# A planned instruction order: keeping small matmul groups together on TensorE, with retuned planner numbers

## The chip, the cores and the metric

One Trainium2 chip, one of its cores. The metric is device time of one execution in microseconds (us); lower is better. The profile's engine names are PE (TensorE matmuls), PEld (its weight loads), DVE (VectorE), ACT (ScalarE), POOL (GpSimd) and SP (SyncE, which issues the DMAs).

## What is computed

A gated linear attention over 4 x 8 heads, 768 steps, head dimension 40, and then two feed-forward layers on the 3072 tokens of width 320 with inner width 2048. Everything is float32. Cut to what matters:

```python
# attention: one recurrence over time for each of the 32 heads
m_new = max(f_t + m, i_t)
C = exp(f_t + m - m_new) * C + exp(i_t - m_new) * outer(v_t, k_t)
n = exp(f_t + m - m_new) * n + exp(i_t - m_new) * k_t
y_t = sigmoid(o_t) * (C @ q_t) / max(|n . q_t|, 1)
# then, on x = y as (3072, 320)
h = x @ w_in          # (3072, 2048)
x = max(0.01 * h, h) @ w_out
h = max(x @ w_in2, 0)
out = (h * h) @ w_out2
```

## The kernel before

The 768 steps are cut into 6 chunks of 128. `attention(c)` does a chunk in closed form for 4 batches b and 2 halves of 4 heads, so 8 groups g = 2b + half. A group on PE is: `mS` (line 635, four 128x128 score products into the one bank `attS`), `mI` (645, the part that comes from the carried state, into the one bank `atty`; not in chunk 0), and `mPV` (651; from chunk 2 on `mPV3`, 657 to 660) into the same `atty`. Around them stand, once a chunk, the gate transposes (546, 547); for each pair of batches the state update `mU` (708, 16 products); for each batch the transpose of the result (750); and in chunk 0 a broadcast of the gates for each group (615). DVE multiplies scores and decay (638), splits operands into high and low parts (665) and combines (684 to 686, which frees `atty`); ACT does the exponentials (626). All these PE pieces are called small groups below: in them a weight tile of 128 columns serves a moving operand of 32 to 128 columns. All other work of PE is called big: `moe_h` (434) and `out1` (465 to 471) for the first layer, `moe_h` and `out2` (513 to 515) for the second. Their moving operand has 256 to 512 columns. Each fp32 product is made of fp32r products of high and low parts, so a block of `moe_h` is 8 matmuls.

The weights of both layers come from DRAM and are split in the kernel (`weight`, lines 387 to 413) by DVE and ACT; the 16 blocks of the first layer are needed from the first chunk on.

The order on every engine is fixed before the run by `Sched`. Each piece is a node with an engine, an estimated duration, a key (how urgent it is), and buffers with a limited number of slots. `forward()` plays the program: each free engine takes, of the nodes that are ready and can have their buffers, the one with the smallest key. `backward()` then replaces keys by latest start times, and this is done 6 times; the best plan is written out. The first keys come from the numbers of the table `ORDER`. When PE has nothing ready, early in the program, the planner inserts a filler: a matmul of zeros with 512 columns (322 writes `hp`, 478 adds zero to an accumulator). Three more products of zeros (461) clear the accumulators.

The choice in `forward()` that the change touches is:

```python
pick = None
for n in sorted(cand, key=lambda n: (n.key, n.seq)):
    if all(b.live or (b.first is n and ...) for b in n.bufs):
        pick = n
        break
```

On the chip each engine then runs its list in order; an instruction whose input is late holds up all behind it on its engine.

Of the kernel before, what the change touches and what calls it, by code (L numbers as in the profile page):

```python
# [30 lines left out]
ORDER = dict(pe0=7000, ld2=80, kv=-2.33, ks=6.4, g2=32.54, z=-15.1, lag=7, m0=0.71, o0=1.85, a04=-6.78, a0s=4.65, a1=29.4, a1s=5.72, a1ld=23.83, w0=-33.49, ws=2.64, bias=1.13, c0=-19.03, cs=13.0, cld=31.54, wl=1.51, outk=2.04)  # L31
SHARE = 0.6
PASSES = 6
# [13 lines left out]
class Node:  # L47
    __slots__ = ("eng", "dur", "fn", "key", "deps", "outs", "ndep", "ready", "allocs", "bufs", "end", "start", "table", "lat", "seq", "alt", "after", "first", "bank")


class Sched:
# [10 lines left out]
    def op(self, eng, dur, key, fn, r=(), w=(), table=None, lat=0, alt=None, after=0):  # L62
# [4 lines left out]
        n.eng, n.dur, n.fn, n.key, n.table, n.lat = eng, dur, fn, key, table, lat  # L67
# [24 lines left out]
        self.nodes.append(n)  # L92
        return n
# [43 lines left out]
    def forward(self):  # L137
# [17 lines left out]
        ready = {e: [] for e in self.SAME}  # L155
# [6 lines left out]
        out, now, dma_free, done, last = [], 0.0, 0.0, 0, 0.0  # L162
        while done < len(self.nodes):

            for e, cand in ready.items():
# [3 lines left out]
                for n in sorted(cand, key=lambda n: (n.key, n.seq)):  # L169
                    if all(b.live or (b.first is n and queue[b.tag][-1] is b and free[b.tag] > 0) for b in n.bufs):  # L170
                        pick = n
                        break
# [25 lines left out]
                dur = n.dur  # L198
                if n.table and n.table != table:
# [63 lines left out]
def mlstm_moe_kernel(  # L263
# [265 lines left out]
    def attention(c, keys, ld):  # L529
# [23 lines left out]
        op("PE", 380, k0, gate_T, r=[(G_sb, f"A{p}"), (G_sb, f"c{p}"), (G_sb, f"w{p}"), (ident, 0)], w=[(gp, 0)])  # L553
# [11 lines left out]
        for b in range(B):  # L565
# [33 lines left out]
            for hf in range(2):  # L599
# [9 lines left out]
                if c == 0:  # L609
# [7 lines left out]
                    op("PE", 4 * 214, key, bc, r=[(ident, 0), (G_sb, "A0"), (G_sb, "c0"), (G_sb, "w0")], w=[(ab, 0)])  # L617
# [19 lines left out]
                op("PE", 4 * (214 if native else 113), key + 0.3, mS, r=tk, w=[(sp, 0)])  # L637
# [3 lines left out]
                if c:  # L641
# [5 lines left out]
                    op("PE", 4 * (214 if native else 113), key + 0.35, mI, r=tk + ([(C32, (b, 0)), (C32, (b, 1))] if native else [(Cst, (b, k)) for k in range(3)]), w=[(py, 0)])  # L647
# [14 lines left out]
                if thirds:  # L662
# [9 lines left out]
                    op("PE", 4 * 126, key + 0.5, mPV3, r=[(pb, (pr, i)) for i in range(3)] + [(vb, (vr, i)) for i in range(3)], w=[(py, 0)])  # L672
                else:
                    op("PE", 4 * 214, key + 0.5, mPV, r=[(aw, 0), (nt, 0)], w=[(py, 0)])
# [25 lines left out]
            if c < NCH - 1 and b % 2:  # L700
# [9 lines left out]
                op("PE", 1170, kU, mU, r=[(x, 0) for _, wv, nt in pair for x in (wv, nt)], w=[(up, 0)])  # L710
# [41 lines left out]
            op("PE", 3 * 112, ko + 0.75, mT, r=[(y, 0), (y, 1), (ident, 0)], w=[(xp, 0)])  # L752
# [106 lines left out]
```

## Time and profile before

| | |
|---|---|
| median of 3 runs | 856.4 us (851.79 to 860.84) |
| the profiled execution | 857.15 us |
| its span, first to last instruction | 855.1 us |
| PE busy in the span | 842.0 us (98%) |
| DVE, ACT, POOL busy | 541.4, 464.9, 77.8 us |
[...]

Attention and the split of the first layer's weights lie in the first 440 us, on top of the first feed-forward layer; from about 440 us on only feed-forward work is left. A busy PE in the profile is not PE at its peak: the ends of matmuls are modelled and overlap the next, so the pace is read from the distance between starts.

### The profile page before, as it was taken

What the parts mean: (1) busy time and instruction counts of PE and PEld (TensorE: products, weight loads), DVE (VectorE), ACT (ScalarE), POOL (GpSimd) and SP (SyncE); (2) the same over time, 40 slices, a digit from 0 to 9 for tenths busy, and PEclk for the clock granted to TensorE, in tenths of its full rate; (3) what the DMA queues carried; (4) which work ended last, traced back from release to release, by engine and by line L of the source; (5) the groups of instructions that cost most, each with busy time, mean ns of one, the idle gap of its engine ahead of it and who ended that gap; (6) DMA issues with size and microseconds to landing.
All of it is one profiled execution on the core that took longest, in us unless ns stands there. A gap on an engine that the chain in (4) does not pass through costs nothing.

```text
span 855.1 us, 14028 instructions
## 1 busy us (share of the span) xinstructions
PE 842.0 (98%) x5310; PEld 729.9 (85%) x5310; DVE 541.4 (63%) x1008; ACT 464.9 (54%) x946; POOL 77.8 (9%) x101
## 2 busy tenths in 40 slices
PE   9899999999999999999999999999999999999998
PEld 7689999788778788788888889999999999999997
DVE  7799876767676776667576899453443443533433
ACT  6577638656765776577455675343333433433332
POOL 2231204103010311011000000000000000000000
PEclk8899999999999999999999999999999999999999
DMA  8675325435343543453232442000000000000000
GB/s 226 222 233 183 118 73 181 140 111 172 103 137 114 165 138 109 152 166 118 77 103 72 165 136 69 1 31 1 1 32 1 14 17 1 31 1 1 32 1 31
DMA packets 52211, 78.60 MB, mean 92 GB/s; under 512 B 4336, under 2 KB 40784, under 8 KB 52144
## 3 DMA queue, kind: packets, MB, share of 16 engines
q1 hardware_dynamic: 52144, 77.71, 28.8%
q8 instruction: 42, 0.69, 0.3%
q14 instruction: 25, 0.20, 0.1%
HBM read 54.26 MB, written 4.01 MB: 68 GB/s over the span
## 4 chain that ended last, share of the span: by engine, by line
PE 82%; DVE 6%; ACT 4%; SPq 3%; DMA 3%; issue 1%; ACTq 0%; DVEq 0%
PE hp L434 36%; PE acc L465 4%; PE acc L467 4%; PE acc L466 4%; SPq L581 3%; PE acc L515 3%; PE acc L514 3%; PE acc L513 3%; PE attS L635 3%; PE acc L470 2%; PE atty L645 2%; PE acc L471 2%; PE atty L651 2%; DMA T<-X 2%; PE atty L515 1%
## 5 line engine op out<-in xcount | busy, mean ns | idle before, releaser
L434 PE MATMUL hp<-xH,w 128*128 128x512 f32 (+1 forms) x1040 | 294.8, 381 | 0.3 <-DVE gL L442 0.3
L434 PEld LDWEIGHTS hp<-xH,w 128*128 128x128 f32 x1040 | 183.5, 189 | 29.2 <-DVE gL L442 0.9
L434 PE MATMUL hp<-xL,w 128*128 128x512 f32 (+1 forms) x624 | 199.1, 375 | 0.0
L446 DVE TENSOR_TENSOR g<-g 128x512 f32<-128x512 f32 x96 | 66.3, 691 | 118.4 <-ACT g L445 118.3
L434 PEld LDWEIGHTS hp<-xL,w 128*128 128x128 f32 x624 | 115.9, 189 | 22.4
L445 ACT ACTIVATE g<-hp 128x512 f32<-128x512 f32 x96 | 57.3, 597 | 129.4 <-PE hp L434 129.4
L448 DVE TENSOR_TENSOR gL<-g,gH 128x512 fp32r<-128x512 f32 x96 | 66.4, 692 | 56.4 <-ACT gH L447 56.4
L447 ACT CAST gH<-g 128x512 fp32r<-128x512 f32 x96 | 59.6, 620 | 70.4 <-DVE g L446 70.4
L442 DVE TENSOR_TENSOR gL<-hp,gH 128x512 fp32r<-128x512 f32 (+1 forms) x112 | 68.3, 610 | 34.7 <-ACT hp L441 34.2
L465 PE MATMUL acc<-gH,w 128*128 128x512 f32 (+1 forms) x224 | 86.1, 384 | 0.0
L440 ACT ACTIVATE gH<-hp 128x512 fp32r<-128x512 f32 (+1 forms) x112 | 59.6, 532 | 48.4 <-PE hp L434 39.3
L467 PE MATMUL acc<-gL,w 128*128 128x512 f32 (+1 forms) x224 | 81.3, 363 | 0.0
L466 PE MATMUL acc<-gH,w 128*128 128x512 f32 (+1 forms) x224 | 81.0, 362 | 0.0
L515 PE MATMUL acc<-w,gL 128*128 128x320 f32 x192 | 59.3, 309 | 0.0
L514 PE MATMUL acc<-w,gH 128*128 128x320 f32 x192 | 59.3, 309 | 0.0
L513 PE MATMUL acc<-w,gH 128*128 128x320 f32 x192 | 59.2, 308 | 0.0
L441 ACT ACTIVATE hp<-hp 128x512 f32<-128x512 f32 (+1 forms) x112 | 59.1, 528 | 0.0
L626 ACT ACTIVATE aw<-aw,cs 128x128 f32<-128x128 f32 x160 | 50.8, 391 | 12.2 <-DMA aw<-Adram 12.1
L629 POOL TENSOR_SCALAR_AFFINE_SELECT aw<-aw 128x512 f32<-128x512 f32 x48 | 33.5, 697 | 196.5 <-ACT aw L626 174.0
L467 PEld LDWEIGHTS acc<-gL,w 128*128 128x128 f32 x224 | 42.6, 190 | 6.9 <-DVE gL L442 0.2
L465 PEld LDWEIGHTS acc<-gH,w 128*128 128x128 f32 x224 | 42.7, 191 | 5.3
L466 PEld LDWEIGHTS acc<-gH,w 128*128 128x128 f32 x224 | 42.8, 191 | 4.9
(163 smaller groups left out, 1515.1 us busy)
## 6 DMA issues: line engine op xcount, KB each, us to landing
T<-X SPq DMA_DIRECT2D x144, 120.0 KB
x<-in_wts_dram SPq DMA_DIRECT2D x16, 704.0 KB
aw<-Adram SPq DMA_DIRECT2D x40, 256.0 KB
nat<-in_nat_dram SPq DMA_DIRECT2D x24, 328.0 KB
qkr<-in_qk_dram SPq DMA_DIRECT2D x16, 360.0 KB
X<-in_wts_dram SPq DMA_DIRECT2D x8, 704.0 KB
T<-in_wts_dram SPq DMA_DIRECT2D x8, 704.0 KB
og<-in_og_dram SPq DMA_DIRECT2D x12, 320.0 KB
```

The lines of the kernel that those rows point to most:

```text
L434: T.matmul(hp.t[:, 0:n], w.t[:, col:col + 128], x.t[:, kt, o], start=(s == 0), stop=(s == 7))
L440: op("ACT", act(n, True), key, lambda: A.activation(gH.t[:, 0:n], h(), AF.Prelu, alpha=0.01), r=[(hp, 0)], w=[(gH, 0)])
L442: op("DVE", dve(n), key, lambda: V.tensor_tensor(out=gL.t[:, 0:n], in0=h(), in1=gH.t[:, 0:n].bitcast(F32), op=ALU.subtract), r=[(hp, 0), ( ...
L446: op("DVE", dve(n), key, lambda: V.tensor_tensor(out=g.t, in0=g.t, in1=g.t, op=ALU.mult), r=[(g, 0)], w=[(g, 0)])
L447: op("ACT", act(n), key, lambda: A.copy(gH.t, g.t), r=[(g, 0)], w=[(gH, 0)])
L448: op("DVE", dve(n), key, lambda: V.tensor_tensor(out=gL.t, in0=g.t, in1=gH.t.bitcast(F32), op=ALU.subtract), r=[(g, 0), (gH, 0)], w=[(gL, 0)])
L465: T.matmul(a[t].t[:, o], w.t[:, hc:hc + 128], gH.t[:, 0:n], start=first, stop=False)
L466: T.matmul(a[t].t[:, o], w.t[:, lc:lc + 128], gH.t[:, 0:n], start=False, stop=False)
L467: T.matmul(a[t].t[:, o], w.t[:, hc:hc + 128], gL.t[:, 0:n], start=False, stop=last)
L513: T.matmul(a.t[:, 0:DM], gH.t[:, s], wH, start=first, stop=False)
L514: T.matmul(a.t[:, 0:DM], gH.t[:, s], wL, start=False, stop=False)
L515: T.matmul(a.t[:, 0:DM], gL.t[:, s], wH, start=False, stop=last)
```

## The change

The planner learns of small groups. Eight `op` calls get `small=True` (all the small groups named above). When a big piece follows a small one, the planner now counts 85 ns more for it. And when the last piece on PE was small and the best candidate is big, the planner goes on through the candidates, up to `STAY` = 3000 ns of key beyond the best, and takes a small one that is ready instead. Beside that, 14 numbers of `ORDER` are different. No instruction's own work changes; the line numbers of the attention part are 8 higher in the changed file.

```diff
-ORDER = dict(pe0=7000, ld2=80, ..., g2=32.54, z=-15.1, lag=7, m0=0.71, o0=1.85, a04=-6.78, a0s=4.65, a1=29.4, a1s=5.72, ..., w0=-33.49, ...)
+ORDER = dict(pe0=7535.6, ld2=74.38, ..., g2=29.83, z=-12.64, lag=5, m0=0.64, o0=2.08, a04=-9.44, a0s=4.65, a1=22.66, a1s=2.23, ..., w0=-42.16, ...)
+STAY = 3000
...
                     if all(b.live or (b.first is n and queue[b.tag][-1] is b and free[b.tag] > 0) for b in n.bufs):
-                        pick = n
-                        break
+                        if pick is None:
+                            pick = n
+                        elif n.small:
+                            pick = n
+                        if e != "PE" or pick.small or not small or n.key > pick.key + STAY:
+                            break
...
                 dur = n.dur
+                if e == "PE":
+                    dur += 85 if small and not n.small else 0
+                    small = n.small
...
-        op("PE", 380, k0, gate_T, r=[...], w=[(gp, 0)])
+        op("PE", 380, k0, gate_T, small=True, r=[...], w=[(gp, 0)])
...
-                op("PE", 4 * (214 if native else 113), key + 0.3, mS, r=tk, w=[(sp, 0)])
+                op("PE", 4 * (214 if native else 113), key + 0.3, mS, small=True, r=tk, w=[(sp, 0)])
```

Over the whole program PE's list has 119 places where a big matmul follows a small group before, and 106 now; products of zeros are 36 before (18 of line 322, 15 of 478, 3 of 461) and 33 now (22, 8, 3).

What this does to the lists is shown at three places. First, PE in chunk 0: the second score product of batch 1, the clearing of accumulators (line 461), fillers (322), and the value product of group 1 (651; the row with `atty` after the fillers). Before:

```order
L651 MATMUL atty<-nat,aw 128x42 x4
L635 MATMUL attS<-w_102 128x128 x4
L635 MATMUL acc_230<-w_105 128x128 x4
L461 LDWEIGHTS warm
L461 MATMUL acc_235<-warm 128x512
L461 LDWEIGHTS warm
L461 MATMUL acc_239<-warm 128x512
L651 MATMUL atty<-nat,aw 128x42 x4
L615 MATMUL attS<-G_sb,ident 128x128 x4
L322 LDWEIGHTS warm
L322 MATMUL hp<-warm 128x512
L651 MATMUL atty<-nat,aw 128x42 x4
```

The same place on PE now (lines are 8 higher: 659 is 651, 643 is 635, 469 is 461, 330 is 322):

```order
L643 MATMUL acc_229<-w_105 128x128 x4
L659 MATMUL atty<-nat,aw 128x42 x4
L469 LDWEIGHTS warm
L469 MATMUL acc_249<-warm 128x512
L330 LDWEIGHTS warm
L330 MATMUL hp<-warm 128x512
L469 LDWEIGHTS warm
L469 MATMUL acc_260<-warm 128x512
L330 LDWEIGHTS warm
L330 MATMUL hp<-warm 128x512
L330 LDWEIGHTS warm
L330 MATMUL hp<-warm 128x512
```

The value product of group 1 moved ahead of the zero products, and these now stand six in a row (one more, of line 486, follows the five shown; then the broadcast 623 and the value product of group 2). Ahead of all work of chunk 0 stand 19 fillers where 16 stood.

Second, DVE in chunk 0, from the normalisation of batch 0 (736 to 743) to that of batch 1; 394, 396 and 399 are three steps of the split of weight blocks 0 (`x_2`) and 1 (`x_3`). Before:

```order
L394 TENSOR_SCALAR x_2_289<-x_4_122 128x704
L738 RECIPROCAL d<-d 128x8
L363 TENSOR_TENSOR G_sb<-G_sb,x_0_74 32x128
L740 TENSOR_TENSOR og<-og,d 128x320
L361 COPY G_sb<-x_0_74 32x128
L743 TENSOR_TENSOR y<-hs,og 128x320
L396 SCALAR_TENSOR_TENSOR x_2_289<-x_4_122,x_2_289 128x704
L736 SCALAR_TENSOR_TENSOR d<-hs 128x8
L399 ISA x_2_289<-x_2_289,wl 128x1408
L756 TENSOR_TENSOR xL<-attm,xH 128x3x128
L737 TENSOR_SCALAR d<-d 128x8
L394 TENSOR_SCALAR x_3_338<-x_5_126 128x704
```

The same place on DVE now (402 is 394, 404 is 396, 407 is 399, 744 to 751 are 736 to 743):

```order
L745 TENSOR_SCALAR d<-d 128x8
L402 TENSOR_SCALAR x_3_291<-x_5_126 128x704
L746 RECIPROCAL d<-d 128x8
L370 TENSOR_TENSOR G_sb<-x_0_74 32x128
L748 TENSOR_TENSOR og<-og,d 128x320
L407 ISA x_2_245<-x_2_245,wl 128x1408
L751 TENSOR_TENSOR y<-hs,og 128x320
L404 SCALAR_TENSOR_TENSOR x_3_291<-x_5_126,x_3_291 128x704
L369 COPY G_sb<-x_0_74 32x512
L744 SCALAR_TENSOR_TENSOR d<-hs 128x8
```

The third step of block 0 and the first two of block 1 moved ahead of the row that starts the normalisation of batch 1 (the last row shown).

Third, PE after the fourth set of gate transposes, where the state update `mU` (708, now 716) stands. Before:

```order
L471 MATMUL acc_2902<-gL,w_386 128x512
L635 MATMUL attS<-T 128x128 x4
L708 MATMUL attm<-wv,nat 40x42 x16
L434 MATMUL hp<-xH,w_583 128x512 x4
L434 MATMUL hp<-xL,w_583 128x512 x2
```

The same place on PE now:

```order
L475 MATMUL acc_2890<-gL,w_406 128x512
L643 MATMUL attS<-T 128x128 x4
L653 MATMUL atty<-Cst,T 128x42 x4
L716 MATMUL attm<-wv,nat 40x42 x16
L643 MATMUL attS<-T 128x128 x4
L478 MATMUL acc_2899<-gH,w_406 128x512
```

Two score products now stand in one cluster with only `mI` and `mU` between them. This form (S, I, U, S) stands 2 times in the list before and 5 times now.

## Rows read from the trace of the kernel before

**Rows 1.** Busy time by stretch: stretch, length, engines (instructions), granted clock, DMA share, GB/s.

```profile
40.00:60.00 20.00, 19.63 (x170) 17.95 (x169) 19.51 (x40) 16.89 (x46) 6.49 (x8) 0.93 0.73 245
60.00:80.00 20.00, 19.70 (x157) 18.68 (x156) 19.63 (x43) 15.79 (x36) 3.58 (x5) 0.99 0.63 198
...
280.00:320.00 40.00, 38.91 (x271) 31.86 (x270) 29.95 (x60) 30.65 (x66) 9.64 (x12) 1.00 0.46 148
...
560.00:600.00 40.00, 40.00 (x225) 36.28 (x224) 17.69 (x27) 14.88 (x27) 0.00 (x0) 1.00 0.05 17
```

**Rows 2.** Timeline of PE, 0 to 36 us: start, duration, operation, count.

```profile
1.05 5.99 PE L322 MATMUL hp<-warm 128*128 128x512 bf16 x16 [1.05 <-DVE warm L319]
6.87 0.24 PE L546 MATMUL attS<-ident,G_sb 96*128 96x96 f32 x1
...
16.30 1.04 PE L461 MATMUL acc<-warm 128*128 128x512 bf16 x2
17.13 1.77 PE L651 MATMUL atty<-nat,aw 128*128 128x42 f32 x8
...
27.26 0.63 PE L478 MATMUL acc<-warm 128*128 128x512 bf16 x1
...
35.39 0.72 PE L434 MATMUL hp<-xH,w 128*128 128x256 f32 x4
```

**Rows 3.** Timeline of DVE, 0 to 36 us; in brackets the idle time before and its releaser.

```profile
5.01 0.28 DVE L363 TENSOR_TENSOR G_sb<-G_sb,x 32x128 f32<-32x128 f32 x1
...
27.83 0.17 DVE L736 SCALAR_TENSOR_TENSOR d<-hs 128x8 f32<-128x8 f32 x1 [3.67 <-ACT hs L682]
27.92 0.88 DVE L399 CUSTOM_DVE_ANT_0 x<-x,wl 128x1408 uint16<-128x1408 uint16 x1
...
29.62 0.52 DVE L394 TENSOR_SCALAR x<-x 128x704 int32<-128x704 int32 x1
...
30.18 0.89 DVE L396 SCALAR_TENSOR_TENSOR x<-x,x 128x704 int32<-128x704 int32 x1
```

**Rows 4.** Timeline of ACT, 7 to 50 us: the exponentials of one group in chunk 0.

```profile
35.73 1.14 ACT L626 ACTIVATE aw<-attS,cs 128x128 f32<-128x128 f32 x4 [1.27 <-PE attS L615]
```

**Rows 5.** Stretches of 1 us, columns as in rows 1.

```profile
15.00:16.00 1.00, 1.00 (x11) 1.00 (x10) 1.00 (x2) 1.00 (x1) 0.32 (x1) 1.00 0.74 234
16.00:17.00 1.00, 1.00 (x5) 0.53 (x4) 1.00 (x2) 0.98 (x3) 0.00 (x0) 0.54 0.65 184
...
29.00:30.00 1.00, 1.00 (x13) 0.25 (x13) 0.92 (x3) 0.72 (x2) 0.00 (x0) 0.63 0.06 23
...
57.00:58.00 1.00, 1.00 (x7) 1.00 (x7) 1.00 (x4) 0.61 (x2) 0.91 (x2) 0.52 0.72 209
```

**Rows 6.** Timeline of PE, 50 to 57 us: first row of a run of small groups, and what follows.

```profile
51.91 0.30 PE L546 MATMUL attS<-ident,G_sb 96*128 96x96 f32 x1
...
56.14 0.74 PE L434 MATMUL hp<-xH,w 128*128 128x256 f32 x4
```

**Rows 7.** Timeline of PE around two small groups at 212 us.

```profile
212.35 0.56 PE L635 MATMUL attS<-T 120*128 120x128 f32 x4
212.75 0.57 PE L645 MATMUL atty<-Cst,T 120*128 120x42 f32 x4
213.16 0.48 PE L465 MATMUL acc<-gH,w 128*128 128x512 f32 x1
213.48 0.39 PE L466 MATMUL acc<-gH,w 128*128 128x512 f32 x1
213.71 0.40 PE L467 MATMUL acc<-gL,w 128*128 128x512 f32 x1
```

**Rows 8.** Who waited for whom, PE, 100 to 460 us: total us, times, longest us.

```profile
PE atty L645 <- DVE hs L686: 2.7, 4, 0.8
PE atty L659 <- DVE x L665: 1.9, 3, 1.3
PE attS L635 <- DVE aw L638: 1.1, 2, 0.8
```

More of the change, by code (lines that the diff above doesn't have):

```diff
@@ L47 @@
 class Node:
-    __slots__ = ("eng", "dur", "fn", "key", "deps", "outs", "ndep", "ready", "allocs", "bufs", "end", "start", "table", "lat", "seq", "alt", "after", "first", "bank")
+    __slots__ = ("eng", "dur", "fn", "key", "deps", "outs", "ndep", "ready", "allocs", "bufs", "end", "start", "table", "lat", "seq", "alt", "after", "first", "bank", "small")
 class Sched:
@@ L60, in buf, with op @@
         return Buf(tag, make)
-    def op(self, eng, dur, key, fn, r=(), w=(), table=None, lat=0, alt=None, after=0):
+    def op(self, eng, dur, key, fn, r=(), w=(), table=None, lat=0, alt=None, after=0, small=False):
         n = Node()
         n.alt, n.after, n.first = alt, max(after, ORDER["pe0"]) if eng == "PE" and key > -2000 else after, (eng, dur, fn)
-        n.eng, n.dur, n.fn, n.key, n.table, n.lat = eng, dur, fn, key, table, lat
+        n.eng, n.dur, n.fn, n.key, n.table, n.lat, n.small = eng, dur, fn, key, table, lat, small
         n.seq, n.outs, n.allocs, n.end = len(self.nodes), [], [], None
@@ L161, in forward @@
                 heapq.heappush(at, (n.after, 1, n.seq))
-        out, now, dma_free, done, last = [], 0.0, 0.0, 0, 0.0
+        out, now, dma_free, done, last, small = [], 0.0, 0.0, 0, 0.0, False
         while done < len(self.nodes):
@@ L645, in mI @@
                             T.matmul(py.t[:, (8 + n) * E:(9 + n) * E], lhs(0, h), st, start=True, stop=True)
-                    op("PE", 4 * (214 if native else 113), key + 0.35, mI, r=tk + ([(C32, (b, 0)), (C32, (b, 1))] if native else [(Cst, (b, k)) for k in range(3)]), w=[(py, 0)])
+                    op("PE", 4 * (214 if native else 113), key + 0.35, mI, small=True, r=tk + ([(C32, (b, 0)), (C32, (b, 1))] if native else [(Cst, (b, k)) for k in range(3)]), w=[(py, 0)])
                 def mPV(py=py, aw=aw, v=v, hd=hd):
@@ L671, in attention @@
                        alt=("POOL", pool(512), lambda lw=lw: lw(G, 1)))
-                    op("PE", 4 * 126, key + 0.5, mPV3, r=[(pb, (pr, i)) for i in range(3)] + [(vb, (vr, i)) for i in range(3)], w=[(py, 0)])
+                    op("PE", 4 * 126, key + 0.5, mPV3, small=True, r=[(pb, (pr, i)) for i in range(3)] + [(vb, (vr, i)) for i in range(3)], w=[(py, 0)])
                 else:
-                    op("PE", 4 * 214, key + 0.5, mPV, r=[(aw, 0), (nt, 0)], w=[(py, 0)])
+                    op("PE", 4 * 214, key + 0.5, mPV, small=True, r=[(aw, 0), (nt, 0)], w=[(py, 0)])
                 def comb(py=py, hs=hs, hf=hf, g=g):
@@ L708, in mU @@
                             T.matmul(up.t[r:r + D, o:o + E], nt.t[:, h * D:(h + 1) * D], wv.t[:, h], start=True, stop=True)
-                op("PE", 1170, kU, mU, r=[(x, 0) for _, wv, nt in pair for x in (wv, nt)], w=[(up, 0)])
+                op("PE", 1170, kU, mU, small=True, r=[(x, 0) for _, wv, nt in pair for x in (wv, nt)], w=[(up, 0)])
                 for i, (b2, _, _) in enumerate(pair):
@@ L750, in mT @@
                     T.transpose(xp.t[:, k * 128:(k + 1) * 128], y.t[:, k * 128:(k + 1) * 128], ident.t)
[L752 removed]
+            op("PE", 3 * 112, ko + 0.75, mT, small=True, r=[(y, 0), (y, 1), (ident, 0)], w=[(xp, 0)])
             xo = slice(b * CH, (b + 1) * CH)
```

6 lines of the change are left out of this document (3 added, 3 removed).

## The prediction

> **What bounds the kernel now.** I read the stretches first, then the timelines of PE, DVE and ACT in the first 36 us, then the list of waits. From 560 to 600 us PE is busy for all 40.00 us while DVE has 17.69 [rows 1]: once attention is over, only the matmuls themselves count, and the change leaves each of them as it was. Time can move in three ways: PE starts its big work earlier or later, it loses less between its instructions, or it waits less for others. The first is decided before 35.39 us, where the first block of line 434 starts [rows 2]; until then PE runs a chain of small groups and zero products. From 40 to 80 us there are two busy engines: PE 19.63 and 19.70 of 20, DVE 19.51 and 19.63 [rows 1]. Waits of PE proper from 100 to 460 us are few: 2.7, 1.9 and 1.1 us in its three largest items [rows 8].
>
> The profiled execution took 857.15 us, 0.75 above the median of 856.4. The sum below goes onto 857.15; 0.75 comes off at the end.
>
> **Boundaries.** In a row of matmuls with 512 columns the starts are 0.23 us apart (213.48 to 213.71). The first one after a small group keeps 0.32 until the next (213.16 to 213.48): 0.09 more [rows 7]. Inside the cluster nothing of the kind shows: the score group takes 0.40 (212.35 to 212.75) and the group from the state 0.41 (212.75 to 213.16), so joining two groups saves one boundary and does not move its price inside. There are 13 boundaries fewer (119 to 106, counted in the lists): 13 x 0.09 = **-1.2 us**, on PE, which sets the end, so nothing hides it. The bounds are 0 (what is saved only lengthens a wait) and -1.2.
>
> [...]
>
> **The start, in four pieces.** (a) The gate chain of chunk 0 is done on DVE at 5.29 us (5.01 + 0.28) [rows 3], but the first transpose starts at 6.87, behind 16 zero products [rows 2]. Three more stand there now. At the full-clock pace of 0.23 that is +0.7 us; the two products from 16.30 to 17.13 took 0.415 each at the lower clock [rows 2], so the upper bound is +1.25. Nothing hides it, since data already waits.
>
> (b) From 16.30 to 27.26 us PE does five zero products and five groups, the last being the value product that ends batch 1 [rows 2]. Now the same five groups have seven products among them, counted to the same place: two more, 0.415 each at the lower clock, **+0.8**.
>
> (c) [...] 10.96 us less five products leave 8.9 us for the groups; a fifth of it is 1.8, and the other four take 7.1. Now six zero products stand in one piece ahead of these four. If the clock came back at their end, the four groups and the product among them would take half: -3.8 us. If it doesn't, 0. I take the middle, **-1.9**, because in the trace it came back after four zero products with a transpose among them, but not after the pair at 16.30, and a return part of the way through the four groups is what lies between these.
>
> (d) DVE idles for 3.67 us before 27.83, waiting for the copy behind that last value product, and then does weight steps of 0.88, 0.52 and 0.89 us that hold up the second half of the input of the first layer [rows 3]. These 2.3 us now stand ahead of the wait, in the idle time. Against that, three other short steps (one of them a normalisation that POOL did) now come before the first big matmul; at about 0.5 us each, as the 0.52 row, they cost 1.5. The exponentials of group 5, 1.14 us on ACT [rows 4], now stand ahead of the cast that the first big matmul needs; behind them wait that cast, DVE's low part and PE. I take **-0.5**; the bounds are -2.3 (the steps cost nothing) and +1.1 (the exponentials in full, no gain).
>
> Sum of the start: 0.7 + 0.8 - 1.9 - 0.5 = **-0.9 us**. It carries to the end if DVE comes along. It does for as long as its own list moves with it: the same steps lie behind it when the first big matmul starts.
>
> **Fillers from 36 to 62 us.** Six zero products stand between the first big matmuls before, one now. Five at 0.23 are 1.15. A filler gone is time gained only if the data comes as much sooner; with DVE at 98% there [rows 1] I take less than half, **-0.5**, bounds 0 and -1.15. On SP the loads of the decay rows and the second part of the gates move past one to three other loads; DMA share is 0.73 and 0.63 from 40 to 80 us [rows 1], so I cost that at nothing; without that room ACT would wait for its decay tiles, and the groups behind them.
>
> **Waits in chunks 2 to 5.** A score group needs the one bank that DVE's product of the group before frees. When the cluster S, I, U, S puts two score groups so close, the second waits: 1.1 us in two waits, the longer 0.8 [rows 8], and the list before has two such clusters. Now it has five. Behind the waiting matmul stands the whole of PE. Three more at 0.55 are +1.65 (bounds +0.9 and +2.4, at 0.3 and 0.8 each). In the other direction, the group from the state waits for DVE to free its bank: 2.7 us in four [rows 8]. Counted in the lists, ten such groups have at most six big matmuls since the value product before them; now three have. I take half of the 2.7 away, -1.35 (bounds 0 and -2.7). The 1.9 us of the split operands I leave. Together **+0.3 us**.
>
> **Sum.** -1.2 - 0.9 - 0.5 + 0.3 = -2.3: 857.15 - 2.3 = 854.85, less 0.75: **854.1 us**. A gain of 0.27%.
>
> **Rivals.** *Slower: the clock.* Clusters of small groups are what went before each fall. From 51.91 to 56.14 us PE did 4.2 us of them without a break [rows 6]; at 57 the clock is at 0.52 [rows 5], and three such microseconds in a row cost 1.5. The list now holds a longer run in chunk 0 (seven groups, S P b P S P and gates, which big matmuls split before) and joined groups in chunk 1 (U S I; S I T P). If the start stays at the lower level (c = 0, +1.9) and two more falls come at 1.5 each, the sum is -2.3 + 4.9 = +2.6: 859.75, less 0.75: 859.0. It decides from the first added fall on: with c = 0 and one fall (+3.4) the gain is already gone. Against it: after 100 us every stretch is at 1.00, like that from 280 to 320 us [rows 1], though clusters stand there too.
>
> *It keeps its clock.* [...] Then the 10.96 us of (b) become 8.9 / 2 + 7 x 0.23 = 6.1, which is -4.9 in place of +0.8 - 1.9; the sum is -6.1: 851.05, less 0.75: 850.3. The row at 16 us speaks against it, with the engine busy 1.00 in the microsecond before. [...]
>
> *It gains nothing beyond the boundaries.* DVE at 19.5 of 20 us from 40 to 80 [rows 1] may set the pace of the weight blocks. Then a sooner start and missing fillers turn into waits of PE for DVE; the start and filler terms go: -1.2 + 0.3 = -0.9: 856.25, less 0.75: 855.5. For it: the fillers from 36 to 62 stood exactly there. Against: PE is as busy as DVE.
>
> **How the numbers follow.** Chances: forecast 0.45, slower by the clock 0.22, nothing beyond the boundaries 0.20, clock kept 0.13. All gains at their bounds give -1.2 + (0.7 + 0.8 - 3.8 - 2.3) - 1.15 + (0.9 - 2.7) = -8.8, or 847.6; all costs 0 + (1.25 + 0.8 + 1.1) + 0 + 2.4 = +5.6, or 862.0. The range, 848.0 to 861.0, leaves out a little on each side. One per cent is 8.6 us, and about what a measurement of this kernel can tell from no change: its three runs lie 9 us apart. Faster by that needs nearly all gains at their bounds (0.09), slower needs some six added falls of the clock or a wait that nothing in the trace announces (0.06); the same 0.85.
>
> **What would show it.** First matmul after a small group 0.09 longer, about 106 times. First transpose at 7.5 us; the clock back at or soon after 22 us instead of 29; the first block of line 434 (442 then) near 34.5. About three more waits of a score group for DVE's product, fewer of the state group. Wrong would be: stretches below 1.00 granted clock after 30 us that together exceed those of before, PE waiting for DVE's weight steps from 35 to 80 us, or a wait on a DMA in the chunks.

## The result, and the profile after

After the change the kernel takes 866.6 us (865.93 to 867.86 in 4 runs); beside it on the same chip the kernel before took 858.4 (851.79 to 860.84). The ratio is 1.0119, interval 1.0084 to 1.0155: slower by 1.2%, outside the range. The profiled execution took 866.4 us. One execution, of the run e4_late below (873.2 us, clock 0.975), counts as slow and is left out of the ratios and means.

The span and mean granted clock of the core, kernel before and kernel after (the clock as a share of full speed):

```profile
core 0: 855.1 us, clock 0.988
...
core 0: 864.7 us, clock 0.976
```

What a clock granted only in part costs is estimated at (1 - clock) x span. This is called the charge below: 10.3 us before, 20.8 after. (For the score group further down that took 2.07 us at 0.50 and 1.16 at 1.00 it gives 1.0 us, where 0.9 were lost.) The difference, 10.5 us, is as large as the whole loss of span, 9.6. What is left of the span without the charge is called the rest: 844.8 before and 843.9 after. (The clock has three decimals, so each charge is good to 0.4 us.)

The charge is taken as an upper estimate, since PE also waits at times (18.92 us busy of 20 from 40 to 60 us). What it is worth can be read from the clock and span of every timed run: among 42 executions of the kernel before, one with 1 us more of charge was 0.69 us longer (standard error 0.09; each is compared with the others of its round). By that, an estimate, the clock accounts for some 7 of the 9.6 us, and about 2 us come from elsewhere. The loss is mostly the clock, but not all of it.

Where the clock was lost: stretches of the kernel after, as in [rows 1] (start and end, length, busy time of PE, PEld, DVE, ACT and POOL with instructions, granted clock, DMA share, GB/s):

```profile
0.00:20.00 20.00, 17.05 (x102) 12.76 (x103) 14.15 (x32) 11.53 (x25) 5.12 (x11) 0.95 0.81 225
20.00:40.00 20.00, 18.83 (x136) 14.97 (x138) 17.58 (x41) 10.08 (x31) 3.04 (x4) 0.80 0.64 200
40.00:60.00 20.00, 18.92 (x99) 17.66 (x98) 14.78 (x29) 11.22 (x29) 4.72 (x5) 0.63 0.54 190
60.00:80.00 20.00, 20.00 (x181) 19.07 (x181) 16.94 (x39) 18.42 (x43) 5.18 (x6) 0.94 0.64 213
80.00:100.00 20.00, 19.48 (x161) 18.83 (x160) 17.90 (x40) 12.02 (x31) 5.05 (x6) 0.83 0.56 176
100.00:120.00 20.00, 20.00 (x178) 19.15 (x177) 19.65 (x44) 13.07 (x33) 5.69 (x7) 0.92 0.39 126
200.00:220.00 20.00, 18.96 (x141) 15.46 (x139) 12.07 (x27) 12.28 (x31) 5.37 (x8) 0.91 0.41 129
560.00:600.00 40.00, 40.00 (x223) 36.20 (x223) 17.83 (x27) 15.48 (x27) 0.00 (x0) 1.00 0.05 17
```

Three of these stretches in the kernel before (the two at 100 and 200 us were at 1.00 there):

```profile
0.00:20.00 20.00, 18.95 (x107) 14.27 (x108) 15.52 (x34) 12.63 (x28) 5.40 (x12) 0.90 0.81 226
20.00:40.00 20.00, 17.82 (x119) 13.38 (x118) 15.79 (x33) 10.19 (x28) 5.13 (x5) 0.76 0.62 202
80.00:100.00 20.00, 20.00 (x172) 18.82 (x172) 17.67 (x41) 11.81 (x29) 4.22 (x5) 0.91 0.50 153
```

From 40 to 60 us the charge is 0.37 x 20 = 7.4 us, against 1.4 before [rows 1]. PE executed 99 matmuls there instead of 170, and DVE went from 19.51 us busy to 14.78, with waits of 2.3 us for ACT and 1.3 us for PE. From 60 to 80 us the charge rose by 1.0, from 80 to 100 by 1.6, from 100 to 120 by 1.6, from 200 to 220 by 1.8. Late in the program nothing moved (40.00 of 40 busy at 1.00, as before).

The timeline of PE in the kernel after, in the three places where the clock falls (start, duration, operation, count, and the idle time ahead with its releaser):

```profile
40.80 1.16 PE L643 MATMUL attS<-w 40*128 40x128 f32 x8 [0.28 <-ACT aw L634]
...
45.35 2.07 PE L643 MATMUL attS<-w 40*128 40x128 f32 x8 [0.47 <-ACT aw L634]
...
51.94 1.20 PE L442 MATMUL hp<-xH,w 128*128 128x256 f32 x4
...
83.33 1.16 PE L643 MATMUL attS<-X 40*128 40x128 f32 x8
...
85.86 1.73 PE L659 MATMUL atty<-nat,aw 128*128 128x42 f32 x8
...
115.40 1.09 PE L659 MATMUL atty<-nat,aw 128*128 128x42 f32 x8
116.32 0.36 PE L473 MATMUL acc<-gH,w 128*128 128x256 f32 x1
116.52 0.28 PE L474 MATMUL acc<-gH,w 128*128 128x256 f32 x1
116.64 0.28 PE L475 MATMUL acc<-gL,w 128*128 128x256 f32 x1
```

A score group takes 1.16 us at 40.80 and 2.07 at 45.35: the granted clock was 1.00 from 41 to 45 us, 0.58 from 45 to 46 and 0.50 from 46 on. From 40.80 us PE runs seven small groups in a row; its list has one zero product behind them and one more value product, and at 51.94 us the first half block of weight block 2 starts. In the kernel before two half blocks, at 43.11 and 45.32 us, and the output products of another stood between such groups:

```profile
43.11 0.72 PE L434 MATMUL hp<-xH,w 128*128 128x256 f32 x4
...
45.32 0.74 PE L434 MATMUL hp<-xH,w 128*128 128x256 f32 x4
```

The rows of the kernel after at 116 us show the boundary too: 0.20 us to the next start for the first big matmul, 0.12 for the following.

Stretches of 1 us of the kernel after:

```profile
45.00:46.00 1.00, 0.65 (x3) 0.65 (x4) 0.48 (x2) 1.00 (x4) 0.63 (x1) 0.58 0.99 400
...
62.00:63.00 1.00, 1.00 (x9) 1.00 (x9) 1.00 (x4) 0.89 (x3) 0.00 (x0) 0.88 0.83 244
```

The low clock lasts from 45 to 62 us (0.50 from 46 on), as long as small groups alternate with single half blocks. Three shorter low stretches follow, at 86 to 92 (0.51), 117 to 120 (0.50) and 205 to 209 us (0.57). Behind 36 us the kernel before has two, that of [rows 5] at 57 to 60 us and one at 84 to 87 (0.68, 0.50 and 0.50 us by us).

Who waited for whom on PE, 100 to 460 us (answers to [rows 8]):

```profile
PE atty L653 <- DVE hs L694: 2.0, 3, 0.9
PE attS L643 <- DVE aw L646: 1.8, 3, 1.0
PE atty L667 <- DVE x L673: 0.7, 1, 0.7
```

### The profile page after: what moved, and what is told of

The parts are those of the page before. It is cut to its first block, busy times and chain, and to the rows that moved or that the text cites. A ratio compares the mean times of both kernels' runs of the same rounds, so it can differ in the third digit from the quotient of the medians.

```text
span 864.7 us, 14030 instructions
## 1 busy us (share of the span) xinstructions
PE 848.9 (98%) x5304; PEld 737.8 (85%) x5307; DVE 537.9 (62%) x1007; ACT 465.8 (54%) x946; POOL 77.5 (9%) x102
## 4 chain that ended last, share of the span: by engine, by line
PE 82%; DVE 8%; SPq 3%; DMA 3%; ACT 2%; issue 2%; DVEq 0%; ACTq 0%
PE hp L442 37%; PE acc L473 4%; PE acc L475 4%; PE acc L474 4%; PE acc L523 3%; PE acc L522 3%; PE acc L521 3%; SPq L589 3%; PE attS L643 3%; PE acc L478 2%; PE acc L479 2%; PE atty L653 2%; PE atty L659 1%; DMA aw<-Adram 1%; PE atty L523 1%
## 5 line engine op out<-in xcount | busy, mean ns | idle before, releaser
L442 PEld LDWEIGHTS hp<-xH,w 128*128 128x128 f32 x1040 | 186.1, 192 | 29.8 <-DVE gL L450 1.7
```

What stands on the lines that cost most here:

```text
L442: T.matmul(hp.t[:, 0:n], w.t[:, col:col + 128], x.t[:, kt, o], start=(s == 0), stop=(s == 7))
```

## The experiments

Each line of this table is one kernel: median of its timed runs, ratio to the kernel before with its interval, from its profiled execution the span, the clock, the charge (1 - clock) x span, and the rest; and in the last column charge and rest as means of its timed runs (for before, of the 42 executions named above). (The ratio is to the kernel before on the same chip, whose median was 855.5 to 858.4 us.)

| kernel | median | ratio | span | clock | charge | rest | means |
|---|---|---|---|---|---|---|---|
| before | 858.4 | 1 | 855.1 | 0.988 | 10.3 | 844.8 | 8.1, 846.0 |
| after | 866.6 | 1.0119 (1.0084 to 1.0155) | 864.7 | 0.976 | 20.8 | 843.9 | 20.3, 844.7 |
| e1_numbers | 865.7 | 1.0108 (1.0067 to 1.0149) | 865.5 | 0.982 | 15.6 | 849.9 | 14.7, 849.7 |
| e4_late | 863.3 | 1.0076 (1.0046 to 1.0105) | 863.3 | 0.981 | 16.4 | 846.9 | 14.7, 846.7 |
| e5_early | 865.6 | 1.0099 (1.0068 to 1.0131) | 863.2 | 0.982 | 15.5 | 847.7 | 15.1, 848.6 |
| e3_zeros | 862.3 | 1.0061 (1.0039 to 1.0084) | 860.5 | 0.990 | 8.6 | 851.9 | 10.8, 849.6 |
| h1_start_of_before | 865.1 | 1.0119 (1.0053 to 1.0186) | 860.6 | 0.982 | 15.5 | 845.1 | 17.3, 846.3 |
| h2_start_of_after | 865.6 | 1.0131 (1.0075 to 1.0187) | 861.8 | 0.981 | 16.4 | 845.4 | 19.9, 844.6 |
| j1_late_blocks | 862.5 | 1.0067 (1.0039 to 1.0095) | 861.0 | 0.982 | 15.5 | 845.5 | 13.9, 846.2 |
| i1_gates_first | 867.6 | 1.0140 (1.0091 to 1.0189) | 865.8 | 0.976 | 20.8 | 845.0 | 20.8, 844.6 |
| e2_grouping | 864.1 | 1.0104 (1.0062 to 1.0146) | 860.4 | 0.984 | 13.8 | 846.6 | 12.1, 849.7 |
| k2_zeros_third | 864.8 | 1.0108 (1.0033 to 1.0183) | 864.8 | 0.986 | 12.1 | 852.7 | 9.1, 853.9 |
| k3_at_most_two | 874.3 | 1.0231 (1.0189 to 1.0272) | 876.0 | 0.975 | 21.9 | 854.1 | 16.4, 856.4 |
| k4_three_old_numbers | 865.4 | 1.0106 (1.0053 to 1.0159) | 865.1 | 0.982 | 15.6 | 849.5 | 10.8, 851.3 |
| s1_spaced_old | 868.5 | 1.0130 (1.0068 to 1.0193) | 867.0 | 0.984 | 13.9 | 853.1 | 10.8, 855.3 |
| s2_spaced_old_2500 | 869.1 | 1.0146 (1.0083 to 1.0209) | 861.8 | 0.998 | 1.7 | 860.1 | 8.3, 858.7 |
| s3_spaced_new | 872.8 | 1.0195 (1.0161 to 1.0228) | 869.6 | 0.984 | 13.9 | 855.7 | 17.2, 854.3 |

**Numbers or grouping.** e1 is the kernel before with the changed table alone; e2 is the changed planner with the old table; e4 and e5 use the grouping only behind or only ahead of 100 planned us.

```diff
 # e1_numbers, on the kernel before: the new ORDER line alone; e2_grouping, on after: the old ORDER line
 # e4_late, on after (e5_early: "now > GROUP" and "now <= GROUP")
+GROUP = 100000
-    if e != "PE" or pick.small or not small or n.key > pick.key + STAY:
+    if e != "PE" or pick.small or not small or now < GROUP or n.key > pick.key + STAY:
-    dur += 85 if small and not n.small else 0
+    dur += 85 if small and not n.small and now >= GROUP else 0
```

e1, expected: 

> The new table of numbers with the old planner (no small groups kept together). In chunk 0 no more than three small groups now stand in a row after the first big matmul; the run of seven (S P b P S P and gates) is gone. Theory A (the loss is TensorE's lower clock level, which follows the long run of small groups): no low stretch from 44 to 62 us, time within 4 us of before, 855 to 862. Theory B (the loss is waits of PE for ACT and DVE that the new numbers bring in the first 100 us): as slow as the changed kernel, 864 to 868, with PE waiting for lines 626 and 638 as in it.

e4, expected: 

> The changed kernel, but groups are kept together only from a planned time of 100 us on; up to there the order is that of the new numbers alone. Theory A: no low stretch from 44 to 62 us; 855 to 862. Theory C (the loss lies in the chunks after 100 us, where joined score groups wait for DVE): still 864 or more, with the waits of line 643 for line 646 of the changed kernel. Theory B: 864 to 868.

e5, expected: 

> The changed kernel, but groups are kept together only up to a planned time of 100 us. The early order on PE is that of the changed kernel, with its run of seven small groups. Theory A: the low stretch from 44 to 62 us stays, 864 to 868. Theory C: 856 to 860, since no cluster S I U S is left.

e2, expected: 

> After's planner, which keeps PE at small groups, with the numbers of before: the grouping alone. Theory A (each long cluster of small groups lowers the clock behind it): this order has no row of seven near 40 us but clusters of four and five later (S I T P and S I u P, from about 75 us on): 857 to 863 us, the loss in stretches at 0.50 that begin behind these clusters. Theory N (only the new numbers do harm): 853 to 857 us.

All four are slower than before, at 1.008 to 1.011. Neither part of the change is harmless, and the losses don't add up to that of both: the numbers alone cost as much as the whole. My expectation that the grouping carries the loss fell with e1. In all four the charge of the profiled execution rose by 3.5 to 6.1 us. In e1 the rest grew by 5.1 as well; in e2 it grew by 1.8 (in the means of all runs by 3.7 in both).

Neither e1 nor e2 has the row of seven. e1 has a row of four at 41 to 47 us, where its expectation had three at most, and its clock fell inside it, at 44 (0.99 from 42 to 44 us, 0.50 from 44 to 46). In e2 the clock was 0.66 from 40 to 60 us, behind a wait of 1.85 us and among three small pieces, and the charge from 40 to 80 us was 10.2 us, more than the 8.6 of after:

```profile
40.00:60.00 20.00, 18.08 (x118) 16.14 (x118) 17.25 (x37) 12.46 (x31) 4.05 (x3) 0.66 0.69 222
```

So a row of seven isn't needed for a fall; whether it is enough for one is the next question.

**Is it the clock.** e3 is the kernel after with 16 zero products at eight joints of small groups from 41 to 54 us, seven of them in and behind the row. j1 is the kernel before in which only PE work of the first layer, with the activations behind it, was put later: loads, weight steps and gate steps stay.

```diff
 # e3_zeros, on after, where the plan is written out; add() is the planner's own filler product
+    if gaps and was and n.small:
+        gaps -= 1
+        for _ in range(2):
+            add()
...
 # j1_late_blocks, on before, where the plan is written out; part is
 # first half blocks 2 and 3 of moe_h with their activations, and out1 of block 1;
 # it goes just ahead of the score group that follows out1 of block 1
...
+    plan[at:at] = part
```

e3, expected: 

> The changed kernel in its own order with two zero products of 512 columns put between each pair of joined small groups, at the first eight such places after the first big matmul: 16 products more, 3.7 us of PE at the full clock. Theory A: granted clock from 44 to 62 us back near 1.0, which gives back about 8 us, less what the products add: 860 to 864, faster with more work. Theories B and C: 866 to 871, slower by what the products add.

j1, expected: 

> The kernel before with one edit of the order: the products of weight blocks 2 and 3 (first half), the activations behind them and the three output products of block 1 are put later, behind the small groups that they stood among, so that six small groups stand in a row from about 40 to 47 us; all loads, weight steps and gate steps stay where they were and are early enough. Theory A1 (the row of small groups alone lowers the clock): a stretch near 0.50 that begins at 44 to 46 us, and 860 to 866 us. Theory A2 (it takes the late weights, not the order of PE): clock as in before, 855 to 859 us.

e3 did 3.7 us more work and was 4.3 us faster than after. The stretch of e3 from 40 to 60 us:

```profile
40.00:60.00 20.00, 19.45 (x170) 16.57 (x171) 15.19 (x33) 14.57 (x38) 3.34 (x5) 1.00 0.60 210
```

The fall is gone, from 60 to 80 us the clock is 1.00 too, and the charge of the whole span is 12.2 us smaller than in after (9.5 in the means of all runs). Added work and gain together, 8.0 us, are about what this charge was worth. In j1 the reverse happened. PE and stretches of j1:

```profile
42.16 1.09 PE L658 MATMUL atty<-nat,aw 128*128 128x42 f32 x8
43.86 1.72 PE L642 MATMUL attS<-w 40*128 40x128 f32 x8 [0.62 <-ACT aw L633]
...
40.00:60.00 20.00, 18.28 (x135) 16.77 (x135) 14.40 (x29) 12.06 (x32) 3.42 (x4) 0.74 0.49 170
60.00:80.00 20.00, 20.00 (x149) 19.04 (x149) 19.62 (x41) 16.97 (x39) 6.08 (x7) 0.91 0.73 232
```

Six small groups in a row, loads and weight steps where they were, and the charge from 40 to 80 us went from 1.6 to 7.0 us; the rest of the span grew by 0.7. Other traces agree: h2, e5 and i1, which have the row of seven, had a charge of 6.8 us each from 40 to 80 us, and three more executions with the start of before (h1, m1, m2) had 1.8, 0 and 0. In j1 the row of small groups in PE's own list was enough to lower the clock (1.00 from 42 to 44 us, 0.57 from 44 to 46, 0.50 to 54). By itself it cost j1 6 us of span, over half of the loss of after.

**One place or several.** h1 and h2 take the first 66 planned us of the one order and everything else of the other.

```diff
 # h1_start_of_before, on after; h2_start_of_after is the reverse
 # first: the nodes that the other order plans to start in its first 66 us, in its order
...
+    return first + [n for n in best[0] if (n.start > UNTIL if n.seq < 0 else n.seq not in done)]
```

h1, expected: 

> The order of before for all that was planned to start in the first 66 us, the order of after for the rest. Theory A (the loss is made in the start, where PE has seven small groups in a row from 40.8 to 51.9 us and its clock falls): 853 to 858 us, at or a little below before, because the later gains (13 fewer boundaries at 0.09 us, 1.2 us) stay; no stretch between 44 and 56 us at 0.50. Theory B (the loss is spread over the later stages by the new numbers): 862 to 867 us, as after.

h2, expected: 

> The reverse: the order of after for the first 66 planned us, the order of before for the rest. Theory A: 863 to 868 us, with the granted clock near 0.50 from 44 to 62 us as in after. Theory B: 855 to 860 us, as before.

Both came out at 865, so the start alone is not it. In h1 the clock from 40 to 60 us was nearly that of before, as expected, but the loss turned up behind it:

```profile
40.00:60.00 20.00, 19.34 (x164) 17.44 (x163) 19.75 (x39) 15.67 (x45) 6.67 (x8) 0.91 0.71 228
...
80.00:100.00 20.00, 19.25 (x112) 18.39 (x111) 13.56 (x33) 8.29 (x21) 2.83 (x4) 0.66 0.51 156
100.00:120.00 20.00, 20.00 (x167) 19.29 (x167) 19.58 (x43) 10.98 (x30) 6.50 (x9) 0.84 0.36 104
```

That is 10.0 us of charge in the clusters from 78 us (state update, S, I, P) and 110 us (S, state update, I, gates, P), where after itself had 5.0. h2 lost it in the row, with a charge of 6.8 us from 40 to 80. So the new order has several places that lose the clock, and what one loses differs with how PE arrives there. Both hybrids' rests (845.1, 845.4) agree with that of before.

**The late load.** In the new order weight block 2 is loaded at 30.23 us instead of 22.87, because DVE's last gate copy, which frees the buffer, stands behind a step that waits. The rows are of DVE and of SP's queue, kernel after:

```profile
28.31 0.17 DVE L744 SCALAR_TENSOR_TENSOR d<-hs 128x8 f32<-128x8 f32 x1 [1.61 <-ACT hs L690]
...
29.99 0.22 DVE L369 COPY G_sb<-x 32x128 f32<-32x128 f32 x1
...
30.23 0.33 SPq L395 DMA_DIRECT2D x<-in_wts_dram  x1
```

I suspected this load next, and i1 moves the gate steps and the load back.

```diff
 # i1_gates_first, on after, where the plan is written out
+    # the last four gate steps and the load of block 2 ahead of the load of block 4
+    plan[at:at] = part
```

i1, expected: 

> After with five rows moved: the last four gate steps of DVE stand ahead of the first division by the normalizer instead of behind the second, and the load of weight block 2, which waits for them, ahead of the loads of blocks 4 and 5. PE's order is that of after. Theory C (the load issued at 30.23 us instead of 22.87 us holds the kernel up by itself): load at 21 to 25 us, and 856 to 860 us. Theory A (PE's own order with its seven small groups is what costs): load as early, time 863 to 868 us, low clock from 44 us as in after.

It changed nothing: 867.6 us, and the first half block of block 2 on PE started at 51.64 us instead of 51.94. DVE's last gate copy in i1 had ended at 23.04 us, 7.2 sooner. The load was not what PE waited for; block 2 is late because PE's list puts it behind the small groups. The idea fell.

**Shorter rows, and more zero products.** k2 is after with 30 zero products ahead of third and later small groups in a row. k3 and k4 limit the length of a row.

```diff
 # k2_zeros_third, on after, where the plan is written out; row counts small groups in a row
+    if row >= 2 and n.small and 38000 < n.start < 225000:
+        for b in n.allocs:
+            if b.bank:
+                for _ in range(2):
+                    T.matmul(b.t, warm.t, zeros(), start=True, stop=True)
 # k3_at_most_two, on after; small is now a count
+    full = small >= MOST            # MOST = 2
...
-    elif n.small:
+    elif n.small != full:
...
-    if e != "PE" or pick.small or not small or n.key > pick.key + STAY:
+    if e != "PE" or pick.small != full or not small or n.key > pick.key + STAY:
...
 # k4_three_old_numbers, on after with the numbers of before
-    if e != "PE" or pick.small or not small or n.key > pick.key + STAY:
+    if e != "PE" or pick.small or not 0 < small < MOST or n.key > pick.key + STAY:   # MOST = 3
```

k2, expected: 

> After with 30 zero products (some 0.23 us each, 6.9 us of added PE work): two ahead of each small group that is third or later in a row and opens a PSUM bank, from 38 to 225 planned us. Theory A: the falls at 45 to 62, 86 to 93, 116 to 120 and 205 to 209 us go; clock loss from 20.6 to 5 to 8 us; 856 to 861 us, faster than after although it does more. If clusters are not what lowers the clock: 868 to 874 us.

k3, expected: 

> The new numbers and a planner that after two small groups in a row prefers a big one (within the same 3 us): behind the first product of a weight block no cluster of three stands in the first 150 us, and there are 111 boundaries, 8 fewer than in before. Theory A: no fall of the clock behind 40 us, clock loss 4 to 8 us, 851 to 857 us. Theory N (the new numbers do the harm whatever the clusters): 862 to 868 us.

k4, expected: 

> The numbers of before and after's planner, which here leaves the rule aside after three small groups in a row: 100 boundaries, clusters of three at most behind 60 us. Theory A: 852 to 859 us, a clock loss between those of the last kernel and of the grouping alone. Theory N: 853 to 857 us.

k2 kept 1.00 from 40 to 80 us, but the falls near 84 and 107 us stayed (0.50 from 84 to 90 us and from 108 to 110); with 6.9 us of zero products its median is 1.9 below that of after, which its runs (858.3 to 870.9) don't tell from nothing. k3 missed by far: in the first 150 us, behind the first weight block, no row is longer than two, and yet the profiled execution, the slowest of its four, has the largest charge of the table. In the mean of all runs the charge is 8.3 above that of before and the rest 10.4, so here other things cost at least as much as the clock. Its timeline of PE:

```profile
38.33 1.16 PE L645 MATMUL attS<-w 40*128 40x128 f32 x8
...
41.67 2.08 PE L625 MATMUL attS<-G_sb,ident 96*128 96x128 f32 x8 [0.74 <-DVE aw L648]
```

A pair, three short big matmuls, a wait, the next pair: the group at 41.67 already takes 2.08 us, where such a group took 1.16 in the kernel before (at 34.48 us, clock 1.00), and the clock is 0.84 from 40 to 42 us and 0.50 from 42 on. The number of groups in a row is not the whole rule, and this kernel could not tell whether the few big matmuls or the wait did it. k4 ended at 865.4, with a rest 4.7 us above before; its fastest run (857.9) had a clock of 0.998.

**The cases by themselves.** Behind the kernel before, a tail of products whose results nothing reads: each case behind 56 big products of 128x512; the second kernel has the cases in reverse order. Only the traces count.

```diff
 # m1_cases and m2_cases_reversed, on before, behind the plan
+    CASES = ['SP', 'SPSP', 'SPSPSP', 'SPSPSPSP', 'SPSPSPSPSPSP', 'ww', 'wwww', 'SPww', 'SPSPwwSP', 'vvvv', 'SoSoSoSo', 'SPoSPoSPo', 'SPBSPBSP']
 # S: 4 products 40x128; P: 4 products 128x42; o: one big, B: eight
 # w: 4 products 128x128 and ScalarE's copy that the next one needs; v: the same for one big
...
```

m1, expected: 

> The kernel before with a tail of products that nothing reads, so only its trace counts: thirteen cases, each behind 56 products of 128x512 (12 us) that should bring the clock to 1.00. Cases in this order: rows of 2, 4, 6, 8 and 12 small groups without a wait; 2 and 4 small groups each of which waits for ScalarE's copy of the one before; 2 groups and 2 waiting ones; 4, 2 waiting, 2; 4 big products that each wait for ScalarE; 4 groups with a big product behind each; 3 pairs with a big product behind each; 2 pairs with 8 big products behind each. Theory A (the length of a row of small groups): falls behind the rows of 6, 8 and 12 and not behind the cases with waits or pairs. Theory W (it takes waits of PE as well, of 0.3 us and more): no fall behind the rows without waits, falls behind the waiting cases.

m2, expected: 

> The same cases in the reverse order, so that a case whose fall hangs on what came before it shows itself: both theories expect the same cases to fall as in the other order.

Timeline of PE in m1, some of the cases:

```profile
882.86 1.16 PE L814 MATMUL attS<-G_sb 40*128 40x128 f32 x8
...
884.86 12.98 PE L807 MATMUL hp<-xH,w 128*128 128x512 f32 x56
897.77 1.16 PE L814 MATMUL attS<-G_sb 40*128 40x128 f32 x8
...
901.87 14.57 PE L807 MATMUL hp<-xH,w 128*128 128x512 f32 x56
916.37 1.16 PE L814 MATMUL attS<-G_sb 40*128 40x128 f32 x8
...
1060.65 1.16 PE L814 MATMUL attS<-G_sb 40*128 40x128 f32 x8 [0.41 <-ACT y L821]
...
1062.65 12.97 PE L807 MATMUL hp<-xH,w 128*128 128x512 f32 x56
...
1148.07 12.97 PE L807 MATMUL hp<-xH,w 128*128 128x512 f32 x56
```

The 56 products after a pair take 12.98 us, at a granted clock of 1.00. After four groups in a row, with no wait anywhere, they take 14.57, and the clock is 0.56 from 902 to 905 us. From start to start, less the same at full pace (2.1 us a pair, the last 2.0, and 12.91 the 56), the rows cost, in m1 and m2: two groups 0 and 0, four 1.6 and 3.2, six 4.7 and 4.8, eight 6.3 and 6.3, twelve 9.3 and 9.5 us. Three pairs with one big product behind each cost 3.2 and 4.7; pairs with eight big products behind each, none. Eight small groups, the fifth and sixth of them 128x128 products, with two waits of 0.35 to 0.41 us (the last of them is the row at 1060.65) cost nothing in both orders; a single score group with one big product behind it, four times, cost 1.6 and 1.5. Big products that waited 0.69 us each lost 1.4 us in one order and nothing in the other. So the falls behind the rows came without a wait, and with one big matmul in between the clock still fell. Theory A is right for the rows of six and more; the fall behind the row of four, those behind pairs and single groups with one big product each, and in one order that behind the waiting big products, are misses of it. Theory W fell: the rows lost the clock without a wait. No case has 128x128 products without waits, so it stays open whether the waits or the wider products kept the clock in the cases with both.

**Spacing by order.** s1 to s3 replace the grouping by its opposite: a count of small work, lowered by big work, sends big groups first while it is high.

```diff
 # s1_spaced_old (DEBT 1700) and s2_spaced_old_2500 (DEBT 2500): numbers of before; s3_spaced_new: new numbers, 2500
-    elif n.small:
+    elif not n.small:
...
-    if e != "PE" or pick.small or not small or n.key > pick.key + STAY:
+    if e != "PE" or not pick.small or debt < DEBT or n.key > pick.key + STAY:
...
+    debt = debt + dur if small else max(0.0, debt - 1.0 * dur)
```

s1, expected: 

> The numbers of before and another planner's rule: PE keeps a count of small work that grows with each small group and shrinks with each big one, and while it stands at 1.7 us or more a big group due within 3 us goes first. 122 boundaries. Theory A2 (the clock falls behind small work that has too little big work between, as in the measured cases): clock loss behind 36 us near 0, 5 to 8 us in all, 851 to 857 us. Theory L (before is simply the order that a search found; any other order loses 4 us or more): 861 to 868 us.

s2, expected: 

> The same with the mark at 2.5 us; 128 boundaries. Theory A2: as the last kernel or 0.5 us above. Theory L: 861 to 868 us.

s3, expected: 

> The same rule at 2.5 us with the new numbers; 114 boundaries. Theory A2: clock loss behind 36 us 0 to 3 us, 852 to 859 us. Theory L: 861 to 868 us.

All three are slower than before, and slower than either theory had them. s2 is the telling one: its profiled execution kept the clock almost throughout (0.998), and was still long, at a rest of 860.1. A stretch of 90 us of s2:

```profile
40.00:130.00 90.00, 84.30 (x715) 77.66 (x718) 79.42 (x171) 57.33 (x139) 19.56 (x22) 0.98 0.50 161
```

PE idles for 5.7 us of these 90; in the kernel before 0.67. What depended on the small groups held back came late. So the spacing bought the clock in this execution, and paid more for it in waits. It didn't buy it each time: of its four timed runs two (863.8 and 864.8 us) had a clock of 0.998 and 0.996, and two (873.3 and 874.0) had 0.984; the rest is 857 to 860 us in all four.

No kernel of this study is faster than the one before.

## Why the prediction was wrong

**Boundaries.** The mechanism was right where the trace shows it: 0.08 us at 116.32, and 13 fewer in the list. That would be -1.0 instead of -1.2; no run times this term by itself.

**The start.** (a) was off: the first transpose starts at 6.72 us, not 7.5, although there are 19 products ahead of it:

```profile
1.05 5.83 PE L330 MATMUL hp<-warm 128*128 128x512 bf16 x19 [1.05 <-DVE warm L327]
6.72 0.25 PE L554 MATMUL attS<-ident,G_sb 96*128 96x96 f32 x1
```

They took 0.30 us each instead of 0.36: in this execution their pace rose sooner (8 matmuls on PE from 3 to 5 us, 6 before; what raised it isn't shown). (b) and (c): the five groups with their zero products took 9.43 us (18.34 to 27.77) instead of 10.96, a gain of 1.5 where the forecast had 1.1; the clock was back at 24 us, not 29 (0.50 from 22 to 24, 0.83 from 24 to 26, 1.00 from 26 to 28), though it fell again from 28 to 31 (0.52 from 28 to 30). No run times the -1.9 us of (c) by itself; that a group takes about half as long at the full clock is shown by the 2.07 and 1.16 us above. Behind them, up to the first block of `moe_h`, 0.85 us were gained against the 0.5 of (d). But these groups began 2.04 us later than before, where (a) had 0.7. So that block started at 35.05 us, 0.34 sooner; the forecast was 0.9. A good part of this is luck of the execution: in five traces with the start of before (before, h1, j1, m1, m2) the block starts between 31.77 and 37.37 us, and in h1 the five groups took 7.87.

What delayed the groups is a wait that the prediction had costed at nothing, under the fillers: the load of the second part of the gates, which moved past others on SP. DVE and PE of the kernel after:

```profile
9.25 0.94 DVE L356 TENSOR_TENSOR_SCAN T<-x,T 32x128 f32<-32x128 f32 x1 [3.98 <-DMA x<-in_gates_dram]
...
14.42 0.67 DVE L646 TENSOR_TENSOR aw<-aw,attS 128x512 f32<-128x512 f32 x1
...
15.14 1.09 PE L659 MATMUL atty<-nat,aw 128*128 128x42 f32 x8 [1.90 <-DVE aw L646]
```

DVE's scan of that part started at 7.83 us before, 1.42 sooner; behind it in DVE's list stands the product of scores and decay, and for that PE's first value product waited 1.90 us. It recurs: the scan started at 8.9 to 9.4 us in five traces with the new start (after, e3, h2, i1, k2), and at 7.4 to 8.7 in the five with the old one. A moved load was looked up by its DMA share and not by who stands in line behind its reader.

**Fillers.** Not to be told apart: the stretch it speaks of was lost to the clock. The list now has two zero products there, not one; the second stands behind the row of seven.

**Waits in chunks 2 to 5.** Score groups waited 1.8 us instead of 1.1 (forecast +1.65), the groups from the state 2.0 instead of 2.7 (forecast -1.35), and the split operands, which I left alone, 0.7 instead of 1.9. Together -1.2 where I had +0.3.

**The step that failed** is the clock behind 36 us. The sum has no term for it, and neither has the upper bound of all costs, 862.0: it stood only in the rival "Slower: the clock", which had the right mechanism and the first place, and the price wrong. The rival took 1.5 us for a fall, from a low stretch of three microseconds, and two more falls. The row of seven that it names began to lose the clock at 45 us, and PE got it back at 62 (0.50 from 46 to 62): from 40 to 80 us the charge was 8.6 us, against 1.6 before, and three more stretches added 5.0. The measured cases show the size that was missing: the price grows with the row, 1.6 to 3.2 us for four groups and 6.3 for eight, because all that is left of the row runs at about half pace (in m1's row of eight 2.08 and 1.93 us a group at a clock of 0.50, instead of 1.16 and 1.09), and the big matmuls behind it start at that clock too (0.50 from 954 to 956 us, 0.76 from 956 to 958). In after the low stretch went on behind the row, over ten microseconds of small groups and single half blocks.

Against the rival I had held that clusters stand after 100 us at 1.00 in the kernel before; the cases explain it as far as they go: pairs with eight big products between them kept the clock (1.00 from 1138 to 1152 us of m1). The chance of 0.06 for slower by one per cent went with this: "some six added falls" were needed at 1.5 each; one long one and a few short ones were enough.

**What stays open.** Which of the orders lose how much is shown in the traces, and e3, j1 and the cases change little but the small and big work on PE. But the kernel as a whole is not predicted by that. e2, k3 and s1 have no row above three where they first lose it behind 40 us (0.66, 0.74 and 0.83 from 40 to 60 us), and in each of them PE had waited just before (1.85, 0.74 and 1.13 us); whether it was the wait isn't shown. Part of the loss of e1, e2, k2 to k4 and s1 to s3 is in their rest, in waits and added products of their own; where the 2 us of after that the clock doesn't account for were lost is not shown, apart from the wait at the start. And theory L of the last runs, that the kernel before is simply an order which suits this chip, and that any other costs 4 us or more, isn't ruled out: no changed order here is faster.

## What to carry to other kernels

Before you put small matmul groups together to save a boundary of 0.09 us each, list the longest rows of them that PE will then run and price each row by what is left of it at half pace once the clock falls, plus the first big matmuls behind it (here a score group took 2.07 us instead of 1.16, and rows of four and eight cost 1.6 to 3.2 and 6.3 us). Look at the granted clock stretch by stretch in the first place: here it explains most of the loss, while waits after 100 us and boundaries moved the way the change meant. And when a reordering is undone in parts, compare the charge and the rest of each part apart, over all timed runs, since the parts of this one don't add up and single executions differ.

## Not expected of the hardware

In m1 the granted clock fell to 0.56 (902 to 905 us) although PE was busy without a break: four groups of fp32 products with 40 rows or 42 columns in a row were enough (56 products behind them 14.57 us instead of 12.98), while behind eight groups with two waits of 0.41 us, and 128x128 products among them, it stayed at 1.00 (1059 to 1065 us). Giving PE 16 more zero products between small groups made the kernel faster (866.6 to 862.3 us).

The same order does not always get the same clock. h1 has the order of before in its start, yet its first 20 us ran at 1.00 instead of 0.90, and its first block of `moe_h` started 3.62 us sooner than in [rows 2]. The traces of m1 and m2, which have the whole list of before, had 0.87 and 0.88 there, and 1.00 from 40 to 80 us. The rows are of h1:

```profile
0.00:20.00 20.00, 18.61 (x119) 13.87 (x120) 15.95 (x36) 13.30 (x32) 5.45 (x12) 1.00 0.82 228
...
31.77 0.72 PE L456 MATMUL hp<-xH,w 128*128 128x256 f32 x4
```
